# The last unit's six half-tile stores: three on each of two queues instead of five and one

## The chip, the core and the metric

The kernel runs on one core of a Trainium2 chip. Its engines run their own instruction streams side by side: TensorE (PE) multiplies matrices into PSUM, VectorE (DVE), ScalarE (ACT) and GpSimd (POOL) work on elements, and SyncE (SP) computes nothing and issues transfers. A transfer between the chip's main memory (HBM) and the on-chip memory (SBUF, 128 partitions) is issued by an instruction in the stream of an engine, here SyncE or ScalarE; the profile calls these streams' issuing parts SPq and ACTq. The issue occupies the stream for a while; the data is then moved by the core's 16 DMA engines, and a semaphore tells when it has landed. The metric is the device time of one execution in microseconds (us), the median of the runs.

## The reference

Eight batches of eight heads, 576 positions, head size 64. First causal attention by blocks of 64 positions, then a gated layer over the 512 features of all heads:

```python
scores = scale * np.matmul(q, k.transpose(0, 1, 3, 2))
mask = block_i >= block_j                      # blocks of 64 positions
attn = softmax(np.where(mask, scores, -1e9))
x = np.matmul(attn, v)                         # heads side by side: (8, 576, 512)
gate_pre[s] = sum over k of conv_w[k] * x[s - 4 + k]     # causal, 5 taps
out = (sigmoid(gate_pre) * (x @ w_val)) @ w_out          # (8, 576, 512), float32
```

## The kernel before

All order is written out by hand: a long list (PLAN) of words, each of which is one step with its indices and, after the sign @, the engine that does it or the PSUM banks that it uses. A word is emitted where it stands, so each engine's stream has its steps in the list's order, and a transfer stands in the stream of the engine that issues it. Waits between engines are put in by the framework from what is read and written.

The attention part goes by pairs of heads: loads, casts, transposes, scores on TensorE, the exponential on ScalarE, masks on GpSimd, the product with the values, normalisation on VectorE, and a transpose that puts the features on the partitions. The gated layer then goes by units n. Units 0 to 7 are the first 512 positions of a batch. The last 64 positions of four batches together make a unit of 256 positions: unit 8 has batches 0 to 3, unit 9 batches 7, 6, 5 and 4 in this order. A unit runs the convolution as matrix products (cn), the gate as a tanh on ScalarE (th), the value product (val), the product of both on VectorE (gv), and then the projection tile by tile: o multiplies on TensorE, oc copies the PSUM bank to an SBUF buffer of osb (ring of five) on the engine named (A is ScalarE, D is VectorE), and st stores it.

Unit 9 is the last in the order of units. It has three tiles. Tile (9,0) is 128 rows by all 512 columns, for batches 7 and 6. Tiles (9,1) and (9,2) are the 128 rows for batches 5 and 4, the first and the last 256 columns. Since the 128 rows of a tile belong to two batches, whose last 64 positions lie apart in the output, each tile is stored by two transfers of 64 rows: h = 0 from partitions 0 to 63 and h = 1 from partitions 64 to 127 (L409 to L412). A half of (9,0) has 128 KB, a half of the others 64 KB. The end of the list reads:

```
o.7.4@3 gv.9.3 o.7.3@0 oc.7.4@A o.9.0@1 oc.7.3@D st.7.4 st.7.3 o.9.2@0 oc.9.0@A o.9.1@2 oc.9.2@D
st.9.0 oc.9.1@A st.9.2 st.9.1
```

So ScalarE copies (7,4), (9,0) and (9,1), VectorE copies (7,3) and (9,2). Tile (7,4) is stored by ScalarE's queue, and of the six transfers of unit 9 only the second half of (9,2); all others are SyncE's. The copies are in line 223 (a helper), the stores of whole tiles in line 407, those of halves in line 411, and the matrix products in line 112 (a helper too). After the last word the program closes (line 497): SyncE waits until all stores have landed, and then the engines meet.

Of the kernel before, what the change touches and what calls it, by code (L numbers as in the profile page):

```python
# [90 lines left out]
def kernel(  # L91
# [10 lines left out]
    nc = tc.nc  # L102
# [286 lines left out]
    def row(n, t):  # L389
        return min(t, {7: 3, 9: 1}.get(n, t))  # L390
# [13 lines left out]
    def store(n, t, m):  # L404
        c, o = cols(n, t), osb[0:128, TILES.index((n, t)) % NO]
        if n < B:
            (nc.scalar if t == 4 else nc.sync).dma_start(out=out[n, 128 * row(n, t):128 * row(n, t) + 128, c], in_=o[:, c])
            return
        for h in range(2):  # L409
            s = n - 8 + 2 * row(n, t) + h  # L410
            (nc.scalar if (n, t, h) == (9, 2, 1) else nc.sync).dma_start(
                out=out[s if n == 8 else 8 - s, 512:SEQ, c], in_=o[64 * h:64 * h + 64, c])  # L412

    def cols(n, t):
        z = t - {7: 3, 9: 1}.get(n, 9)
        return slice(256 * z, 256 * z + 256) if z >= 0 else slice(0, 512)
# [16 lines left out]
    def warm(m):  # L433
# [5 lines left out]
        "wv": scale_w_val, "wo": cast_w_out, "tq": trans, "Lqr": load_first, "cqr": cast_first, "tqr": trans_first, "kz": ends, "s": scores, "e": exps,  # L439
        "m": mask, "av": av, "n": norm, "xtr": xtrans, "xd": xtrans_dma, "xt": evac_x,  # L440
        "cn": conv, "th": gate, "val": val, "gv": gated, "o": proj, "oc": evac_out, "st": store,
        "cw": taps, "cT": evac_taps, "DG": diags, "w": warm, "Lcn": load_conv,
    }
# [58 lines left out]
```

## Time and profile before

| what | us |
|---|---|
| median of 3 runs (lowest, highest) | 171.03 (170.67, 171.23) |
| the profiled execution | 171.92 |
| its span, from the first to the last instruction | 170.13 |
| TensorE busy | 158.8 (93%) |
| VectorE, ScalarE, GpSimd busy | 127.8, 125.7, 98.8 |
| stores of 64 rows on SyncE's queue | 9 (5 of them unit 9's), median 0.587 an issue |
| stores of 64 rows on ScalarE's queue | 1, 0.530 an issue |

The mean granted TensorE clock is 0.981. All times in the views are counted from the start of the span. In the timeline a line gives the start, the duration, the engine, the line of the program, the operation, what it writes and reads, and how many instructions were merged; the idle time ahead of it and what ended that stand in brackets. For SPq and ACTq the duration is that of the issue, not of the transfer. In the windows the columns are the length, the busy time of PE, PEld, DVE, ACT and POOL (with their numbers of instructions), the granted clock, the busy share of the DMA engines and the GB/s they moved. A row of 40 digits shows a stretch in 40 equal slices, in tenths of busy time.

### The profile page before, as it was taken

The page shows a single profiled execution, that of the slowest core. Times are in us where ns is not written, and L with a number is a line of the kernel's source. Part 1 is how long each engine was busy: PE and PEld are TensorE (multiplying, and loading weights), DVE is VectorE, ACT ScalarE, POOL GpSimd, SP SyncE. Part 2 cuts the span into 40 slices and gives each one's busy share as a digit, 9 for nine tenths or more (in the row PEclk, how much of TensorE's full clock was granted, in tenths as well). Part 3 has the DMA queues.
Part 4 walks back from the last instruction along what each step waited for, and adds up shares of the span by engine and source line. Part 5 has one row for each costly group of instructions (what it writes and reads, how often), then busy time and mean ns, then how long its engine had stood idle before and what let it go on. Part 6 is the DMA issues. An engine that isn't in the chain of part 4 may idle for free.

```text
span 170.1 us, 7366 instructions
## 1 busy us (share of the span) xinstructions
PE 158.8 (93%) x3121; PEld 102.0 (60%) x3121; DVE 127.8 (75%) x271; ACT 125.7 (74%) x155; POOL 98.8 (58%) x190
## 2 busy tenths in 40 slices
PE   7769999999999999999989999999999999999970
PEld 2346877567675666587556766656756558454550
DVE  3884789879699989888986778766999459729540
ACT  5499999898886999789775897768787971440330
POOL 5279999996969469939760799265672362000000
PEclk9995999999999999999999999999999999999996
DMA  5999999999999605999798969993899899564554
GB/s 187 369 335 396 368 323 319 338 337 365 305 284 390 162 0 139 284 302 322 216 250 312 262 117 235 310 300 84 206 296 230 181 126 173 128 233 185 191 193 116
DMA packets 56027, 41.97 MB, mean 247 GB/s; under 512 B 46005, under 2 KB 46517, under 8 KB 55994
## 3 DMA queue, kind: packets, MB, share of 16 engines
q1 hardware_dynamic: 55770, 41.31, 85.3%
q8 instruction: 24, 0.39, 1.0%
q10 hardware_dynamic: 224, 0.20, 0.3%
q14 instruction: 9, 0.07, 0.1%
HBM read 30.42 MB, written 9.44 MB: 234 GB/s over the span
## 4 chain that ended last, share of the span: by engine, by line
PE 80%; ACT 5%; DMA 4%; DVE 3%; POOL 2%; issue 1%; SPq 1%; POOLq 0%; DVEq 0%
PE B L112 76%; ACT pt L278 5%; DMA qks<-in_q_dram 4%; PE B L315 3%; DVE x L308 1%; DVE xt L328 1%; SPq L174 1%; POOL qk L223 1%; DVE w_val L231 1%; DVE qT L239 0%; POOL v16t L220 0%; POOL v L217 0%; DVE rc L307 0%; POOL pt L286 0%; ACT osb L223 0%
## 5 line engine op out<-in xcount | busy, mean ns | idle before, releaser
L278 ACT ACTIVATE pt<-B 128x1024 f16<-128x1024 f32 x96 | 92.0, 1029 | 12.7 <-PE B L112 11.7
L223 POOL CAST qk<-qks 128x1152 f16<-128x1152 f32 (+2 forms) x31 | 41.3, 1343 | 10.4 <-DMA qks<-in_q_dram 5.5
L112 PEld LDWEIGHTS <-pt 128*128 128x128 f16 x960 | 34.2, 98 | 8.3 <-issue 1.9
L112 PE MATMUL B<-v,pt 128*128 128x65 f16 x896 | 36.4, 194 | 2.0 <-issue 1.0
L112 PE MATMUL B<-xt,w_val 128*128 128x512 f16 (+1 forms) x160 | 35.8, 359 | 0.4 <-DVE x L308 0.4
L112 PE MATMUL B<-w_out,gv 128*128 128x512 f16 (+1 forms) x152 | 36.2, 368 | 0.0
L112 PE MATMUL B<-qT,kT 32*128 32x448 f16 (+3 forms) x640 | 34.0, 292 | 2.1 <-DVE qT L239 1.1
L308 DVE TENSOR_TENSOR x<-B,rc 128x320 f16<-128x320 f32 x64 | 31.5, 492 | 2.4
L384 DVE SCALAR_TENSOR_TENSOR gv<-th,B 128x512 f16<-128x512 f32 (+1 forms) x40 | 24.5, 630 | 8.1 <-PE B L112 5.0
L372 ACT ACTIVATE th<-B 128x1024 f32<-128x1024 f32 (+1 forms) x20 | 17.7, 941 | 16.2 <-PE B L112 9.7
L112 PEld LDWEIGHTS <-kT 32*128 32x128 f16 x640 | 18.5, 93 | 16.4 <-issue 11.1
L112 PEld LDWEIGHTS <-w_val 128*128 128x128 f16 x160 | 14.0, 98 | 14.0 <-issue 2.1
L217 POOL CAST v<-vst 128x512 f16<-128x512 f32 x32 | 19.6, 618 | 4.0 <-PE B L112 1.7
L239 DVE STREAM_TRANSPOSE kT<-qk 128x576 f32<-128x576 f32 (+2 forms) x17 | 19.6, 1160 | 1.5 <-POOL qk L223 1.5
L112 PEld LDWEIGHTS <-gv 128*128 128x128 f16 x152 | 13.4, 98 | 11.0 <-issue 0.8
L239 DVE STREAM_TRANSPOSE qT<-qk 128x576 f32<-128x576 f32 (+3 forms) x18 | 19.4, 1103 | 0.4 <-POOL qk L223 0.3
L307 DVE RECIPROCAL rc<-B 128x5 f32<-128x5 f32 x64 | 11.8, 184 | 10.4 <-PE B L112 10.0
L286 POOL MEMSET pt<- 64x384 f16 x32 | 13.3, 414 | 9.8 <-ACT pt L278 8.1
L223 DVE COPY osb<-B 128x512 f32<-128x512 f32 (+1 forms) x21 | 13.7, 658 | 6.3 <-PE B L112 6.2
L285 POOL COPY pt<-pt 128x128 f16<-128x128 f16 x32 | 9.6, 301 | 13.2 <-ACT pt L278 12.8
L223 ACT COPY osb<-B 128x512 f32<-128x512 f32 (+1 forms) x17 | 9.5, 574 | 7.8 <-PE B L112 4.4
L112 PE MATMUL B<-xt,DG 32*32 32x512 f16 (+1 forms) x800 | 13.1, 356 | 0.0
(45 smaller groups left out, 112.6 us busy)
## 6 DMA issues: line engine op xcount, KB each, us to landing
qks<-in_k_dram SPq DMA_DIRECT2D x16, 576.0 KB, 6.3
qks<-in_q_dram SPq DMA_DIRECT2D x16, 576.0 KB, 6.8
vst<-in_v_dram SPq DMA_DIRECT2D x64, 128.0 KB, 5.4
out_dram<-osb SPq DMA_DIRECT2D x31, 256.0 KB, 3.1
vtst<-in_v_dram SPq DMA_DIRECT2D x8, 128.0 KB, 6.7
th<-in_moe_w_val_dram SPq DMA_DIRECT2D x2, 512.0 KB, 7.1
osb<-in_moe_w_out_dram SPq DMA_DIRECT2D x2, 512.0 KB, 5.7
out_dram<-osb SPq DMA_DIRECT2D x7, 128.0 KB, 2.4
```

Of the source, the lines that this page charges most:

```text
L112: nc.tensor.matmul(out=out, lhsT=lhsT, rhs=rhs, start=start, stop=stop, skip_group_check=True)
L217: nc.gpsimd.tensor_copy(out=v16s[p % NV][0:128, 0:4, 0:2, 0:64], in_=vst[p % NVS][0:128])
L223: (eng.copy if eng is nc.scalar else eng.tensor_copy)(out=o, in_=i)
L239: nc.vector.transpose(out=(qT, kT)[i][a % NQT][0:128].bitcast(fp32).rearrange("p c (x n) -> p c n x", n=9)[:, :, x // 2:y // 2], in_=qk16[ ...
L278: nc.scalar.activation(out=pts[(2 * a + r) % NPT][0:128, 0:2, 512 * t:512 * t + 512], in_=two(bank["s", a, t, 2 * r], bank["s", a, t, 2 * ...
L285: nc.gpsimd.tensor_copy(out=pt[0:128, 0:2, 1536:1600], in_=pt[0:128, 0:2, 0:64])
L286: nc.gpsimd.memset(pt[64:128, 0:2, 0:1536].rearrange("p h (t s) -> p h t s", t=3)[:, :, :, 0:64], 0.0)
L307: nc.vector.reciprocal(out=rc[0:128], in_=O[:, :, 64:65])
L308: nc.vector.tensor_tensor(out=x16[p % NX16][0:128, 0:5, h, 0:64], in0=O[:, :, 0:64], in1=rc[0:128].to_broadcast([128, 5, 64]), op=ALU.mult)
L315: nc.tensor.transpose(out=f16(m[0])[:, 128 * i:128 * i + 128], in_=x16[p % NX16][0:128, i, 0:2, 0:64], identity=ident16[0:128, 0:128])
L372: nc.scalar.activation(out=ths[ORDER.index(n) % NTH][0:128, 2 * r:2 * r + 2, 0:w], in_=two(bank["cn", n, 2 * r], bank["cn", n, 2 * r + 1], w),
L384: nc.vector.scalar_tensor_tensor(out=gvs[z % NG][0:128, x, 0:w], in0=ths[z % NTH][0:128, x, 0:w], scalar=1.0, in1=f32(bank["val", n, x])[: ...
```

## The change

```diff
         for h in range(2):
             s = n - 8 + 2 * row(n, t) + h
-            (nc.scalar if (n, t, h) == (9, 2, 1) else nc.sync).dma_start(
+            (nc.scalar if n == 9 and h else nc.sync).dma_start(
                 out=out[s if n == 8 else 8 - s, 512:SEQ, c], in_=o[64 * h:64 * h + 64, c])
```

The list stays the same. For unit 9 every first half (partitions 0 to 63) is now issued by SyncE and every second half (partitions 64 to 127) by ScalarE. The streams of TensorE, VectorE and GpSimd do not change. The ends of the other two become:

| stream | before | after |
|---|---|---|
| SyncE | (9,0) h0, (9,0) h1, (9,2) h0, (9,1) h0, (9,1) h1 | (9,0) h0, (9,2) h0, (9,1) h0 |
| ScalarE | copy (9,0), copy (9,1), (9,2) h1 | copy (9,0), (9,0) h1, copy (9,1), (9,2) h1, (9,1) h1 |

## The prediction, made before the result was known

> **What bounds the kernel now.** I read the page's slices first. TensorE is busy in all but the end, and only the last two of 40 slices (4.25 us each) thin out; the change lies there and nothing ahead of it is touched. Then the chain of waits over the last 15 us, which says where computing stops, then the timeline of ScalarE's and SyncE's queues in windows that hold one instruction each.
>
> ```profile
> PE   7769999999999999999989999999999999999970
> ...
> DMA  5999999999999605999798969993899899564554
> ```
> ```profile
> 154.88 9.95 PE B L112 x135
> 164.83 0.02 issue
> 164.86 0.37 ACT osb L223
> ```
> ```profile
> 163.09 0.38 ACTq L407 DMA_DIRECT2D out_dram<-osb  x1
> 163.98 0.58 ACT L223 COPY osb<-B 128x512 f32<-128x512 f32 x1 [0.93 <-PE B L112]
> 164.86 0.37 ACT L223 COPY osb<-B 128x256 f32<-128x256 f32 x1 [0.29 <-PE B L112]
> 164.92 0.53 ACTq L411 DMA_DIRECT2D out_dram<-osb  x1
> ```
> ```profile
> 164.59 0.48 SPq L411 DMA_DIRECT2D out_dram<-osb  x1
> 165.13 0.59 SPq L411 DMA_DIRECT2D out_dram<-osb  x1
> 165.81 0.55 SPq L411 DMA_DIRECT2D out_dram<-osb  x1
> 166.45 0.55 SPq L411 DMA_DIRECT2D out_dram<-osb  x1
> 167.05 0.59 SPq L411 DMA_DIRECT2D out_dram<-osb  x1
> ```
>
> The last compute, ScalarE's eviction of tile (9,1), ends at 165.23. The span ends at 170.13, so 4.9 us belong to stores alone. SyncE issues its five back to back from 164.59 to 167.64; from the second on, none waits for data, since every eviction is over before 165.3. What sets the end is the fifth issue (start 167.05), its way to landing (2.1 us by the window that holds it alone, 169.11) and 1.02 us of closing work. Does the data path also limit? The windows by rate:
>
> ```profile
> 161.77:162.47 0.70, 0.70 (x9) 0.63 (x7) 0.69 (x3) 0.00 (x0) 0.00 (x0) 1.00 1.00 372
> 164.45:164.95 0.50, 0.37 (x4) 0.09 (x1) 0.40 (x1) 0.21 (x2) 0.00 (x0) 1.00 0.74 250
> 165.72:166.34 0.62, 0.00 (x0) 0.00 (x0) 0.00 (x0) 0.00 (x0) 0.00 (x0) 1.00 0.97 203
> 165.72:167.48 1.76, 0.00 (x0) 0.00 (x0) 0.00 (x0) 0.00 (x0) 0.00 (x0) 0.90 0.90 224
> 168.28:168.74 0.46, 0.00 (x0) 0.00 (x0) 0.00 (x0) 0.00 (x0) 0.00 (x0) 0.50 0.64 143
> ```
> ```profile
> DMA  9970000000699988799994992018850049710000
> ```
>
> The last two columns are the DMA engines' busy share and GB/s. A store of 128 rows moves 372 GB/s; the 64-row store of 128 KB moves 203 at the same business. The single row is the 40 slices of 164.5 to 169.2: the engines start at about 165.7, are busy until about 167.5, and then show two holes ahead of the last two stores. The end waits for issues; the stretch before it is full.
>
> **The change part by part.** It removes nothing. Two issues leave SyncE, second halves of (9,0) and (9,1); ScalarE carries both and keeps that of (9,2).
>
> SyncE: its three issues take the places of the first three of before, 164.59, 165.13 and 165.81, provided that the third, (9,1), has its data by 165.81 (below). Saved on this queue: 167.05 − 165.81 = 1.24 us.
>
> ScalarE: the first added store waits for that engine's own eviction of (9,0), over at 163.98 + 0.58 = 164.57; it starts at about 164.59, as SyncE's does. A 64-row issue there took 0.53 us (the only such row), so it ends at 165.12. Queued behind it is the eviction of (9,1), which started at 164.86: it now starts at about 165.14, 0.28 later, and ends at 165.51. Both stores of (9,1) wait for that. SyncE's queue is not free for its one until 165.72, so 0.2 us of cover is left; if ScalarE's issue grew beyond about 0.75 us the cover would be gone and each further 0.1 us would delay both last stores by 0.1. ScalarE's second issue, (9,2), goes beside that eviction, as in before (164.92 against 164.86): 165.20 to 165.73. The third waits for the queue and starts at about 165.78. Both queues' last issues therefore start at about 165.8.
>
> Landing: the last one took 2.06 us (167.05 to 169.11). Now two 64 KB stores travel at once behind fuller engines. From below: one 128-row store of the same 128 KB took 1.7 from issue to landing (SyncE, issued 163.57), 0.3 less. From above: lone stores of 64 KB show 0.46 us of transfer, so one wholly behind the other adds about 0.5; a backlog from the earlier ones is the second rival. I take +0.2, nearer to the 64-row rows, whose long issues these are, and keep −0.3 to +0.5. Then 165.81 + 2.06 + 0.20 = 168.07 against 169.11: **1.04 us less**. The closing work is unchanged: SyncE waits for all landings in either version. The moved waits on semaphores of older stores are for transfers issued by 161.55, which land in 2.1 us, before 164.6, and cost nothing.
>
> The profiled execution took 171.92 us, 170.13 of span and 1.79 around it; it becomes 170.88. It stands 0.89 above the median of the three runs, 171.03; less 1.04 that gives **170.0 us**.
>
> A rule that speaks against the change stands in the Trainium skill, SBUF — State Buffer, section "Can I just issue two DMAs to hit both halves?": two concurrent transfers, one at partition 0 and one at 64, measured 6% above one, since all run on the same engines. By it the rate would be an estimated 203 × 1.06 = 215 GB/s, six stores 2.44 us from 165.72, and the time 170.45. No run shown so far has opposite halves started together; the trace agrees that half-tiles move slower than whole ones (203 against 372).
>
> **The rivals.**
>
> *The data path is the bound.* If opposite halves share the engines no better than the stores of 165.72 to 167.48 did (224 GB/s, 0.90 busy, with one ScalarE store among SyncE's), 524,288 bytes take 2.34 us from 165.72, to 168.06; last packet to landing was 0.37 (168.74 to 169.11), so 168.43, a gain of 0.68 and 170.35 us. For it speaks that this stretch was as busy as it gets; against it that the rate of whole tiles was 372, and that opposite halves may mix into that.
>
> *The queues take turns.* If a store's issue on one queue holds up the other's, the six issues of before in a row (0.48, 0.53, 0.59, 0.55, 0.55 and 0.59) last 3.29 us: from 164.59 to 167.88 instead of 167.64, 0.24 later, with nothing gained elsewhere: 171.03 + 0.24, of which the filled small gaps between issues (0.05 to 0.09 each) give a little back: 171.2 us. Against it: at 164.92 to 165.45 ScalarE's issue ran beside two of SyncE's (0.48 and 0.59), and neither is longer than a lone one at 146.10 (0.59). Here the change would not do what it says.
>
> *Slower: ScalarE's sequencer stalls in an issue and takes the eviction with it.* Issues on SyncE grew to 1.56 us (138.21) and 2.07 (123.77) where DMA engines were full. The eviction of (9,1) now stands behind such an issue, and the third issue behind two. With i for one issue the last start is 164.59 + 2i + 0.12; it reaches 167.05 at i = 1.17 us, where the gain is gone. At 1.56 it is 167.83, 0.78 late: 171.8 us. For it: the first two issues now start at the same instant, just as the engines fill. Against it: every 64-row issue of the trace, with full engines too, took 0.48 to 0.60.
>
> **How the numbers follow.** 0.50 for the forecast, 0.27 for the data path, 0.10 for turns, 0.13 for the stall. The forecast's own range is 169.5 (landing at −0.3, so 1.54 less) to 170.3 (landing at +0.5, so 0.74 less). The range of 8 in 10 runs from 169.5 over the data path's 170.35 to the turns' 171.2, and leaves out the stall and a little below. 0.3% of 171.03 is 0.51 us, about what a measurement can tell from no change. Faster by more: 0.48 of the forecast and 0.20 of the data path, whose 0.68 is near that bound: 0.68. Within: 0.02 + 0.07 + 0.09 = 0.18. Slower: 0.13 + 0.01 = 0.14.
>
> **What the next profile would show.** Three L411 issues on SyncE starting near 164.6, 165.1 and 165.8; three on ScalarE near 164.6, 165.2 and 165.8, each of 0.48 to 0.6; the 128x256 copy on ScalarE at about 165.14; no holes in the DMA row between 165.7 and the end; the last landing at about 168.1. Wrong, if copies or issues on ScalarE are longer or start after 165.5 (stall), if issues alternate between the queues (turns), or if the DMA row stays full at 200 to 230 GB/s past 168.0 (data path).

## The result and the profile after

The changed kernel takes 170.18 us (median of 20 runs, 169.54 to 171.31) against 170.88 for the kernel before in as many runs. The ratio is 0.9953, with a 95% interval of 0.9930 to 0.9975: 0.8 us less. The forecast was 170.0, a ratio of 0.9940. Some executions fall into a slower state, here one of the 20 of before (177.85 us), which the ratios leave out; the first of the two runs with equal halves below was profiled in it.

The profiled executions, 170.13 and 168.30 us of span, differ by more than the change did. In the changed one the first store of unit 9 is issued at 163.52 instead of 164.59, and nothing ahead of it was touched: this 1.07 us is scatter of one execution. So from here on times are counted from that first issue. From it to the end of the span it is 5.53 us before and 4.77 after, 0.76 less, which agrees with the ratio. This count is far steadier than a whole run: in both traces ScalarE's copy of (9,0) starts 0.610 and 0.611 us ahead of zero and VectorE's copy of (9,2) 0.173 and 0.174.

The timeline of SyncE's queue in the changed kernel, instruction by instruction, then that of ScalarE and its queue:

```profile
163.52 0.48 SPq L411 DMA_DIRECT2D out_dram<-osb  x1
164.09 0.55 SPq L411 DMA_DIRECT2D out_dram<-osb  x1
164.73 0.55 SPq L411 DMA_DIRECT2D out_dram<-osb  x1
```
```profile
163.53 0.54 ACTq L411 DMA_DIRECT2D out_dram<-osb  x1
164.16 0.37 ACT L223 COPY osb<-B 128x256 f32<-128x256 f32 x1 [0.67 <-PE B L112]
164.19 0.74 ACTq L411 DMA_DIRECT2D out_dram<-osb  x1
164.96 0.62 ACTq L411 DMA_DIRECT2D out_dram<-osb  x1
```

SyncE's three issues start at 0, 0.57 and 1.21 (forecast: 0, 0.54 and 1.22). ScalarE's first is as forecast too (0.54), but its second takes 0.74, and so the third starts at 1.44, not 1.19. Its landing, the last of all, comes at 3.76 (before: 4.52).

The windows by rate over the same stretch (length, busy times, clock, DMA share, GB/s), and the DMA row and its GB/s in 40 slices of 0.1175 us from 0.09 ahead of the first issue, as for the kernel before:

```profile
164.62:166.70 2.08, 0.00 (x0) 0.00 (x0) 0.00 (x0) 0.00 (x0) 0.00 (x0) 0.87 0.88 252
164.62:165.24 0.62, 0.00 (x0) 0.00 (x0) 0.00 (x0) 0.00 (x0) 0.00 (x0) 1.00 0.95 195
165.24:166.70 1.46, 0.00 (x0) 0.00 (x0) 0.00 (x0) 0.00 (x0) 0.00 (x0) 0.81 0.86 277
```
```profile
DMA  9970000000599996999997879983000000000000
GB/s 340 349 236 26 0 0 0 0 0 0 139 227 192 192 209 139 314 436 349 349 323 236 236 201 305 270 236 114 0 0 0 0 0 0 0 0 0 0 0 0
```

The two holes of before are gone: the engines work from slice 10 to 27 without a break, 2.08 us instead of 3.0. The first 0.62 us move at the rate of a single half-tile (195, before 203): although two stores were issued 5 ns apart, one of them travels alone. What comes behind goes at 277.

The packet records of the trace say when each store's first packet starts (on each queue, the packets with data in order of start, one for each row of a store). Here they are with the end of the issue ahead of them (end of issue → first packet), for some of the kernels that follow too, in us from the first issue:

| kernel | SyncE's stores | ScalarE's stores | last packet ends |
|---|---|---|---|
| before | 0.48→1.14, 1.12→1.92, 1.76→2.46, 2.40→3.06, 3.04→3.70 | 0.85→1.74 | 4.14 |
| before, half the columns | 0.48→1.13, 1.12→1.77, 1.76→2.42, 2.40→3.05, 3.04→3.69 | 0.81→1.46 | 3.99 |
| changed | 0.48→1.13, 1.12→2.06, 1.76→2.44 | 0.55→1.73, 1.40→2.24, 2.06→2.84 | 3.21 |
| changed, half the columns | 0.48→1.13, 1.12→1.77, 1.76→2.41 | 0.53→1.44, 1.40→2.06, 2.05→2.72 | 3.02 |
| changed, half the rows | 0.34→0.84, 0.81→1.31, 1.28→1.78 | 0.38→1.15, 0.85→1.45, 1.33→1.90 | 2.18 |
| four stores | 0.48→1.14, 1.14→2.19 | 0.85→1.74, 1.50→2.52 | 3.00 |

A store of 64 rows that nothing holds begins its packets 0.65 us after its issue has ended, whether a row has 512, 1024 or 2048 bytes.

### The profile page after: what moved, and what is told of

Read it like the earlier page. It is cut to its first block, busy times and chain, and to the rows that moved or that the text cites. A ratio compares the mean times of both kernels' runs of the same rounds, so it can differ in the third digit from the quotient of the medians.

```text
span 168.3 us, 7366 instructions
## 1 busy us (share of the span) xinstructions
PE 158.2 (94%) x3121; PEld 101.4 (60%) x3121; DVE 127.4 (76%) x271; ACT 125.7 (75%) x155; POOL 99.0 (59%) x190
## 4 chain that ended last, share of the span: by engine, by line
PE 80%; ACT 8%; DVE 5%; DMA 2%; issue 2%; ACTq 0%; DVEq 0%
PE B L112 77%; ACT pt L278 7%; PE B L315 3%; DMA qks<-in_k_dram 2%; DVE qT L239 1%; DVE x L308 1%; DVE xt L328 1%; ACT osb L223 1%; DVE w_val L231 1%; DVE kT L239 0%; DVE qk L223 0%; ACTq L411 0%; DVE rc L307 0%; ACT kz L223 0%; DVEq L307 0%
```

## The experiments

Two theories were set against each other. Issues: the end is the start of the last issue, plus its landing. Data path: the six stores' transfer sets the end, whoever issues them. A third came up on the way: a stage ahead of the packets that both queues share and that takes one store at a time.

**Each half of the change alone.** The condition in line 411 is replaced:

```diff
-            (nc.scalar if n == 9 and h else nc.sync).dma_start(
+            (nc.scalar if (n, t, h) in ((9, 0, 1), (9, 2, 1)) else nc.sync).dma_start(
```

> Only the second half of (9,0) moves to ScalarE; both halves of (9,1) stay on SyncE, so SyncE issues four. Counted from the start of the first store of unit 9 to the end of the span (5.53 us before, 4.77 in the changed kernel). Theory of issues: the fourth SyncE issue starts 1.8 us after the first, lands 2.1 later and 1.0 of closing follows: 4.9 us, a gain of 0.6 over before. Theory of the data path: 512 KB at the 252 GB/s of the changed kernel need 2.1 us from the first packet, 1.1 us after the first issue, then 0.4 to land and 1.0 to close: 4.6 to 4.8, as in the changed kernel.

```diff
-            (nc.scalar if n == 9 and h else nc.sync).dma_start(
+            (nc.scalar if (n, t, h) in ((9, 1, 1), (9, 2, 1)) else nc.sync).dma_start(
```

> Only the second half of (9,1) moves; (9,0) stays whole on SyncE, and ScalarE's copy of (9,1) has no store ahead of it. Same count as in the run with only (9,0) moved. Theory of issues: fourth SyncE issue at 1.85 us, so 4.95 us, a gain of 0.6 over before. If both single moves gain 0.6 and the two together 0.76, the two gains are not independent: the second is mostly taken by something else than issues. Theory of the data path: 4.7 to 4.8 us.

Measured: 4.88 and 4.89 us from first issue to end, gains of 0.65 and 0.64; the ratios were 0.9967 (0.9935 to 1.0000) and 0.9976 (0.9947 to 1.0004). SyncE's fourth issue starts at 1.82 and 1.85, and its packets begin 0.66 and 0.73 after that issue has ended, so that they wait for little but the issue. With one store moved, issues set the end. Both gains together would be 1.29, the changed kernel has 0.76: the second move finds something else in its way.

**All six on SyncE.**

```diff
-            (nc.scalar if n == 9 and h else nc.sync).dma_start(
+            nc.sync.dma_start(
```

> All six stores of unit 9 on SyncE. Theory of issues: one more issue than before on the queue that sets the end, 0.6 us more than before from first store to end: 6.1 us. Theory that the queues take turns anyway: as before, 5.5 us.

Measured: 6.16 us, 0.63 more, the last issue at 3.09. The ratio of 1.0018 (0.9990 to 1.0046) is too coarse to show it, the trace is not. One 64-row store on SyncE costs 0.63 of the queue.

**The copy behind ScalarE's store.** In the list, the copy of (9,1) goes to VectorE:

```diff
-st.9.0 oc.9.1@A st.9.2 st.9.1
+st.9.0 oc.9.1@D st.9.2 st.9.1
```

> The changed kernel with the copy of (9,1) on VectorE instead of ScalarE, so that no copy stands behind a store's issue. VectorE is free at that time and would end it 0.2 us earlier. Theory that the delayed copy and ScalarE's queue set the end: 0.1 to 0.25 us less than the changed kernel from first store to end (4.5 to 4.65). Theory of the data path: the same 4.77 within 0.05.

Measured: 4.64 us, ratio 0.9949 (0.9913 to 0.9985). The copy ended 0.27 earlier, at 0.74, and ScalarE's second store was issued at 0.56 instead of 0.67 (the first issue of unit 9 stands at 163.93 in this trace):

```profile
164.50 0.84 ACTq L411 DMA_DIRECT2D out_dram<-osb  x1
```

But that issue then took 0.84 and ended at 1.40 as before, and the last packet ended at 3.22 (3.21 in the changed kernel). The 4.64 lies in the range of the first theory, but not by its mechanism: the 0.14 us that the end moved lie behind the last packet, 0.08 in its landing and 0.06 in the closing, where two waits of SyncE follow the last landing instead of three. So the copy was no limit, and ScalarE's second issue is not slow by itself: it waits for something that comes free at 1.40, whether it starts at 0.56, 0.65 (with only (9,0) moved) or 0.67.

**Bytes.** The six stores take only the first half of their columns (the other outputs of unit 9 are left out), in the changed kernel and in the one before:

```diff
+        if n == 9:
+            c = slice(c.start, c.start + (c.stop - c.start) // 2)
         for h in range(2):
```

> The changed kernel with each of unit 9's six stores cut to the first half of its columns (the rest of those outputs is left out): the same issues and copies, half the bytes. From the first of them to the end of the span (4.77 us in the changed kernel). Theory of the data path (the 512 KB of 2.08 us hold back ScalarE's packets, and through them its second issue): 256 KB let ScalarE's first packet start well before 1.73, its second issue falls from 0.74 to about 0.55, and the end comes 0.4 to 0.7 earlier: 4.1 to 4.4. Theory that the queues take turns in issuing, whatever the bytes: ScalarE's second issue stays at 0.74 and the end at 4.6 to 4.75, less only by the shorter last transfer.

> The kernel before with the same cut to half the columns (the rest of those outputs is left out). Its end was set by the fifth issue on SyncE, with holes in the DMA row ahead of it. Theory that issues set the end there: issues unchanged (last start 2.45 after the first), only the last transfer is shorter, 0.1 to 0.2: 5.3 to 5.45 us from first store to end against 5.53. If the data path had set it, 4.9 or less.

Measured: before 5.39 us, its issues unchanged (the last at 2.45): issues set its end, as forecast. The changed kernel fell to 4.41, between the two theories: half the bytes took 0.2 us off the packets (last end 3.02), and the last landing came 0.38 behind its last packet instead of 0.55. But ScalarE's second issue stayed at 0.75 and ended at 1.40 again. Here are that issue (the first of unit 9 stands at 163.81) and the DMA row of the run, in the same slices:

```profile
164.46 0.75 ACTq L413 DMA_DIRECT2D out_dram<-osb  x1
```
```profile
DMA  9960000000399986744713725500000000000000
```

From slice 16 on the engines are far from full, so bytes do not hold these stores. The table shows where they wait. SyncE's three go at their own pace, an issue every 0.64 and packets 0.65 behind its end, as in the kernel before. ScalarE's do so too, but 0.30 behind: its first store was issued at 0.00 and its packets came at 1.44 and not at 1.18, and its second issue ended 0.28 after SyncE's second, its third 0.29 after SyncE's third. In the kernel before with the same cut, ScalarE's store was issued 0.28 later and its packets came only 0.03 later (1.46), 0.65 behind its issue, with no wait. So a store of 64 rows seems to occupy something that both queues share for 0.2 to 0.3 us; whoever comes second within that time waits, and stays behind.

The held issue shows this, the first packets do not. On each queue one 64-row issue ends about 0.64 after the other; ScalarE's second ended 0.87 after its first here and 0.86 in the changed kernel, 0.2 too late whatever the bytes. Where ScalarE's first store is issued 0.32 after SyncE's (the two last experiments), its second issue ends 0.64 to 0.65 after its first and is not held. The first packets of the two queues, 0.30 apart here and 0.60 in the changed kernel, would come about by the engines alone: 64 packets on 16 engines are four each, by estimate 4 × 72 ns = 0.29 us here and 4 × 157 ns = 0.63 us there, the time that SyncE's first store keeps the engines busy.

**Rows.** The same bytes in half as many rows, 32 of 64 with all columns (the others are left out):

```diff
-                out=out[s if n == 8 else 8 - s, 512:SEQ, c], in_=o[64 * h:64 * h + 64, c])
+                out=out[s, 512:SEQ, c] if n == 8 else out[8 - s, 512:544, c], in_=o[64 * h:64 * h + (64 if n == 8 else 32), c])
```

> The changed kernel with each of unit 9's six stores cut to the first 32 of its 64 rows (the rest of those outputs is left out): the bytes of the run with half the columns, in half as many rows. Theory that the shared stage works by rows: first packets of successive stores 0.15 to 0.2 apart instead of 0.3, ScalarE's second issue below 0.6, end at 4.1 to 4.25. Theory that it costs a fixed 0.3 per store: first packets 0.30 to 0.36 apart again and the end at 4.35 to 4.45, as with half the columns.

Measured: 3.68 us, last packet at 2.18. The issues took 0.34 to 0.44, ScalarE's second 0.35 with no wait (the first issue of unit 9 stands at 165.01):

```profile
165.51 0.35 ACTq L411 DMA_DIRECT2D out_dram<-osb  x1
```

On both queues the second issue ended 0.47 after the first, and SyncE's packets began 0.50 after an issue instead of 0.65. Halving the bytes of each row had left the issues, this delay and the held issue as they were; halving the rows shortens the first two, and the third is gone. So what a store costs ahead of its packets goes with its rows. ScalarE's first packets came 0.31 behind SyncE's, the figure of the theory of a fixed cost, but two packets of 156 ns on each engine give 0.31 too (an estimate), so this distance doesn't speak for it; the later pairs came 0.14 and 0.12 apart, instead of 0.29 and 0.30. With the same bytes the packets took 1.34 us here and 1.88 with half the columns. The end came earlier than either theory said, because neither had counted that the issues themselves would be shorter.

**Opposite halves.** Both halves of each tile are read from partitions 0 to 63 (the second half's rows get the first's values):

```diff
-                in_=o[64 * h:64 * h + 64, c])
+                in_=o[0:64, c] if n == 9 else o[64 * h:64 * h + 64, c])
```

> The changed kernel with both halves of every tile of unit 9 read from partitions 0 to 63 (the second half's rows get the first half's values): same bytes, issues and queues, but never opposite halves in flight. Theory that the two halves of a tile, started together on two queues, mix into the rate of a whole tile: without that the 2.08 us of data grow towards 2.5 (203 GB/s), and the end from 4.77 to 5.0 to 5.2. Theory that the two queues' stores are served one after the other on each engine, so that opposite halves gain nothing: 4.77 within 0.05.

> The kernel with both halves of every tile read from partitions 0 to 63 once more. If opposite halves in flight together move faster than equal ones: from first store to end 5.2 to 5.3 again, with the later stores' packets at 80 ns instead of about 50. If the first look was off for a reason that lies outside the stores: 4.8.

Measured: 5.27 and 5.28 us, last packet at 3.88. The DMA row and GB/s of the second of these runs, in the same slices:

```profile
DMA  9970000000699994998996999979899961000000
GB/s 340 349 236 18 0 0 0 0 0 0 139 227 192 209 261 105 262 227 174 192 235 122 192 192 210 209 148 253 157 201 218 192 131 18 0 0 0 0 0 0
```

The engines are busy without a break and move 191 GB/s, against 252 in the changed kernel. With the stores of the two queues reading opposite halves, the last packet ends 0.67 us earlier. ScalarE's first store shows it best: with 2048 bytes a packet took 85 ns on average in the changed kernel and 156 with equal halves. The half alone does not do it: with all six stores on SyncE the second half of (9,0), behind the first on the same queue, took 147 ns a packet. Why the queue matters here stays open, and how a division by whole tiles would fare was not run. ScalarE's second issue ended at 1.40 here too.

**An earlier first store.** The copy of (9,0) is divided by columns between ScalarE and VectorE:

```diff
+        if (n, t) == (9, 0):
+            for e, x in ((nc.scalar, 0), (nc.vector, 256)):
+                copy(e, osb[0:128, TILES.index((n, t)) % NO, x:x + 256], f32(bank["o", n, t])[:, x:x + 256])
+            return
         copy(eng, osb[0:128, TILES.index((n, t)) % NO, c], f32(bank["o", n, t])[:, 0:c.stop - c.start])
```

> The changed kernel with the copy of (9,0) divided by columns between ScalarE and VectorE (256 each), so that the first two stores start earlier. The copy of 512 columns took 0.59, that of 256 on ScalarE 0.37 and on VectorE 0.42: the first store starts about 0.18 us earlier against the last matmul. Theory of the data path: everything behind shifts with it, from the last matmul to the end of the span 4.55 becomes about 4.37, and the median falls by 0.2. Theory of ScalarE's copy of (9,1) as the limit: no change, since that copy still waits for the last matmul.

The two copies did not run side by side: VectorE's began 0.03 us after ScalarE's had ended and waited for it, so the first store came 0.25 us later against the last matmul, not earlier; ratio 0.9978 (0.9948 to 1.0008). What an earlier first store brings was not tested by this. From the first issue on, this run is the changed kernel's end once more: 4.80 us, last packet at 3.25, ScalarE's second issue ending at 1.40.

**Fewer stores.** (9,2) is copied into the buffer of (9,1), beside its columns, and each half of 64 rows goes as one store of 512 columns: two stores on each queue. ScalarE's copy of (9,1) stands ahead of its first store. The order of stores is now, in place of lines 409 to 412 for unit 9:

```diff
-        copy(eng, osb[0:128, TILES.index((n, t)) % NO, c], f32(bank["o", n, t])[:, 0:c.stop - c.start])
+        copy(eng, osb[0:128, TILES.index((9, 1) if (n, t) == (9, 2) else (n, t)) % NO, c], f32(bank["o", n, t])[:, 0:c.stop - c.start])
...
+        if n == 9:
+            if t == 2:
+                put(nc.scalar, 0, 1, slice(0, 512))
+                return
+            put(nc.sync, t, 0, slice(0, 512))
+            if t == 1:
+                put(nc.scalar, 1, 1, slice(0, 512))
+            return
...
+    def put(eng, t, h, c):
+        o = osb[0:128, TILES.index((9, t)) % NO]
+        eng.dma_start(out=out[7 - 2 * t - h, 512:SEQ, c], in_=o[64 * h:64 * h + 64, c])
```

> Unit 9 with four stores instead of six: tiles (9,1) and (9,2) are copied into one buffer and each half of 64 rows by 512 columns goes as one store; on ScalarE the copy of (9,1) stands ahead of its first store. Theory of a stage that both queues share and that serves one 64-row store at a time (first packets 0.30 to 0.36 apart in the run with half the bytes, whatever the queue): two turns fewer; ScalarE's first store, issued 0.3 later, still starts its packets at about 1.73; the second pair is issued at about 0.7 and 0.9, and the last packet ends at about 2.95 instead of 3.2: from first store to end 4.5 to 4.6 against 4.77. Theory that bytes alone set it: 512 KB as before, 4.75 to 4.85, since the last bytes are issued no earlier.

Measured: 169.36 us, ratio to the kernel before 0.9913 (0.9883 to 0.9944); 4.22 us from first issue to end, last packet at 3.00. ScalarE's issues took 0.53 and 0.55. Its windows:

```profile
165.13:165.75 0.62, 0.00 (x0) 0.00 (x0) 0.00 (x0) 0.00 (x0) 0.00 (x0) 1.00 0.96 202
165.75:167.01 1.26, 0.00 (x0) 0.00 (x0) 0.00 (x0) 0.00 (x0) 0.00 (x0) 1.00 0.93 317
```

The last packet came near the first theory's 2.95, but the end came earlier than either theory said. Behind the first store the same bytes as in the changed kernel move at 317 GB/s, not 277, with the engines 0.93 busy instead of 0.86. All four issues are over at 1.50, and the second pair's packets begin 1.0 us behind their issues, not 0.65: here it is the engines that the stores wait for. Of the 0.56 us gained on the changed kernel, 0.21 are packets, 0.19 a shorter landing of the last store (0.36 behind its last packet instead of 0.55) and 0.16 the closing: SyncE waits for the semaphores in a fixed order, 0.065 us each, and here the last to land stands last in it, while in the changed kernel three waits follow. Why the last landing took 0.55 there stays open; it was 0.54 in the run with the divided copy and 0.35 to 0.49 in all others.

**The copy first, with six stores.** The same order on ScalarE, but six stores (put is as above, with the tile's row in place of t):

```diff
+        if n == 9:
+            put(nc.sync, t, 0, c)
+            for x in {0: (), 2: (0, 2), 1: (1,)}[t]:
+                put(nc.scalar, x, 1, cols(9, x))
+            return
```

> The changed kernel's six stores and queues, with ScalarE's copy of (9,1) ahead of its first store, as in the run with four stores: so only the number of stores tells the two apart. Theory that the four-store gain (4.22 us from first store to end against 4.77) came from fewer and longer stores: here 4.65 to 4.8, the last packet at 3.2 as in the changed kernel. Theory that it came from the copy no longer standing behind a store: 4.2 to 4.4.

Measured: 4.68 us, last packet at 3.31; ratio 0.9922 (0.9887 to 0.9957), whose interval overlaps that of four stores. ScalarE's first issue came at 0.32 instead of 0.005, and its first packet at 1.76 instead of 1.73: the early issue had bought nothing. Its second issue took 0.55, not 0.74, and yet ended at 1.49 (the first issue of unit 9 stands at 163.49):

```profile
164.43 0.55 ACTq L421 DMA_DIRECT2D out_dram<-osb  x1
```

So fewer and longer stores, not the copy's place, made the packets end earlier with four. Which of the two counts, the number of stores or the longer rows of 2048 bytes, these runs do not separate.

## Why the prediction was right, and where it was not

The direction and the mechanism held: issues on SyncE set the end before (half the bytes left them and the end almost where they were), and two of them moved to ScalarE shorten it. SyncE's three starts came within 0.04 us of the forecast, the third within 0.01. The saving was 0.76 in place of 1.04.

The term that was mis-sized is ScalarE's chain of three issues. The step counted 0.53 to 0.59 for each, independent of SyncE's, with the last starting 1.19 after the first and over at 1.72; it started at 1.44 and was over at 2.06. ScalarE's first store was issued together with SyncE's, and its queue then stayed about 0.3 behind: its second issue was held until 1.40. Of the 0.28 us that the saving fell short, 0.22 are this later start (1.44, where 1.22 was said for the later of the two queues). The other 0.06 are the way to landing, 2.32 from issue to landing where 2.26 was said. That the +0.2 came out so close was luck in part: the wait for the other stores' packets took 0.12, and 0.17 came from a landing of 0.55 behind the last packet, where 0.38 was seen before and no reason was given for more; the issue itself was 0.03 longer, the packets 0.07 shorter. The delay of the copy of (9,1), to which the forecast gave much room, cost nothing: two runs had it earlier, and the last packet ended at 3.2 to 3.3 as before.

The rival of the queues taking turns was dismissed because two overlapping issues of before were no longer than lone ones. That row could not show it: ScalarE's store came 0.32 us after SyncE's, a distance at which the later runs saw no hold. Something like turns is real, but it costs about half of what the rival gave it (0.3 instead of 0.55 to 0.59), so two queues with an issue every 0.64 each still fit beside each other, one 0.3 behind.

The data path as a rival gave 170.35, as near to 170.18 as the forecast's 170.0. So the time alone does not tell the two apart; the experiments do. The rival's rate, 224 GB/s, was too low (252), and half the bytes saved no more than 0.2 us at the last packet.

The rule of the Trainium skill, SBUF — State Buffer, section "Can I just issue two DMAs to hit both halves?", that two transfers at partitions 0 and 64 together are only 6% faster than one, does not hold for these six. The trace agrees with it only in that the first pair's packets started one behind the other, with 195 GB/s in the first 0.62 us. Over all six the rate was 252 GB/s, 24% above the 203 of one, and with equal halves throughout the packets took 2.75 us, with opposite ones 2.08. The stall that would have made the kernel slower did not come: the copy of (9,1) started 0.64 after the first store, 0.09 later than said, and no issue exceeded 0.74. One sign that the forecast had named for the stall did come, an issue on ScalarE longer than 0.6, but its cause was the hold just told, and it stayed far below the 1.17 at which the gain would have been gone.

## What to carry to other kernels

When the last microseconds are a row of short stores on one queue, with holes in the DMA row between them, a second queue can take the holes out, but count on less than the issues taken away add up to (0.76 of 1.24 us here): the second queue was held for 0.2 us when both began at once, and its last store waited 0.12 us for packets of the others. Once the holes were closed here, fewer and longer stores brought more: two pairs of 64 rows with 512 columns ended their packets 0.2 to 0.3 us before three pairs, some with 256, and the whole 0.46 to 0.56 us before, with the closing and the landing in it. The intervals of their whole times overlap. Compare such versions from a marker behind the untouched part to the end, since the rest of the execution scatters by more than the change.

## What the runs showed of the hardware that was not expected

Two 64-row stores issued within 5 ns on two queues start their packets 0.60 us apart with 2048 bytes a row and 0.30 apart with 1024, and the later queue's next issue is held until 1.40 us after the first, so that it lasts up to 0.84 us; 0.32 us apart, nothing is held. Distances between 0.005 and 0.28 us were not run. Half-tiles of opposite halves on two queues moved 252 GB/s, the same stores with equal halves 191. In the kernels with opposite halves an issue not held took 0.34 to 0.44 us for 32 rows, 0.48 to 0.62 for 64, and 0.33 (SyncE) for 128 rows of the same 128 KB, less than for 64. The end of the program also depends on which semaphore the last store has: SyncE waits for them in a fixed order, 0.065 us each. Which unit takes the stores in turn, and why 64 rows cost more to issue than 128, these runs don't tell.
